# Positions loaded in two halves and loads reordered in the prologue of a Hyena filter with a maxout FFN

## The chip, the cores and the metric

The kernel runs on one core of one Trainium2 chip. The metric is the device time of one execution in microseconds (us), lower being better. All arrays are float32.

## The reference

The program is a Hyena long convolution followed by a feed-forward layer with three maxout branches. B = 4, S = 12544, D = 128, filter order 64, hidden width 768.

```python
h_filt = (np.maximum(pos_emb @ w1, 0.0) @ w2) * np.exp(-0.01 * pos)[:, None]
u = x * v
y = irfft(rfft(u, 2 * S) * rfft(h_filt, 2 * S), 2 * S)[:, :S]       # along the sequence
x = (x * y).reshape(B * S, D)
h = np.maximum(np.maximum(x @ moe_w1, x @ moe_w2), x @ moe_w3)
out = h @ moe_w_out
```

`pos_emb` is 12544 x 64. The decay, `exp(-0.01 pos)`, is zero in float32 from position 82 x 128 on, so only the first NH = 82 blocks of 128 positions (two halves of HH = 41 blocks) enter the filter.

## The kernel before

The program is written out by hand: the order of the calls in the source is the order of the instructions on each engine, and a tile's reader waits for its writer. Its stages are:

- a **prologue**, which makes the filter's hidden layer: relu of positions times w1, times the decay;
- 16 **quads** that transform four hidden channels each, then 32 quads that transform the units of batch 0, with the raw double-precision FFN weights turned into float32 on VectorE beside them;
- the filter's spectrum, stored to DRAM, and batch 0's convolution;
- a main loop of the FFN over tiles of batch 0, 1 and 2, with the convolution of the next batch in between, and a last stage for batch 3.

The change lies in the prologue. What happens there, with lines of the kernel before:

- **Positions.** `pos` (in the memory of `specH`) has 128 partitions: 64 filter inputs for the first 41 blocks and, below them, the same 64 for the other 41. Eight loads (L290 to L295), in pieces of 10 or 11 whole blocks, alternate between SP's and ACT's queues. Each partition's piece is one run of 5 KB or more.
- **Small constants on POOL's queue** (L282 to L289): the decay `win`, `eye`, the reversal `back`, and w1 twice (`w1_sb`).
- **Warm-up** (`warm_up`, L299): TensorE multiplies zeros, 22 rounds and later 3 more. One round is two matmuls, which the trace records as four.
- **The window** (`window_back`, L305): TensorE transposes `win` by `eye`; ACT copies it to `winT` in four pieces; TensorE multiplies by `back`, which reverses and splits it into even and odd positions; ACT copies the result to `winr`.
- **The relu groups** (loop at L903): `mlp_in(i)` (L321) is 32 matmuls into one of two PSUM tiles `pm`, for 16 of the 128 positions of every block, beginning with the highest. Groups 0 to 3 take positions 127 to 64, groups 4 to 7 take 63 to 0. `mlp_out(i)` (L333) is two VectorE instructions per group, relu times `winr`, and frees that `pm` for group i + 2. One relu-group matmul gives two records in the trace, so a group is 64 records.
- **Units.** `u_load` (L349) brings 4 channel rows of x and v (two loads of 196 KB in runs of 392 B) on SP's queue, `u_mul` (L359) multiplies them on VectorE, and `turn2` (L877) transposes two units on TensorE (`pst`), with one ACT copy (`uT`). Units 0 and 1 are turned behind group 7.
- **Raw FFN weights.** `load_raw` (L198) fills one of two buffers `raw` with half a weight matrix; `convert` (L211) is a list of 12 VectorE instructions, dealt out by `some` (L863) between the quads. The first two halves are loaded by SP, the others by POOL.
- **Order on SP's queue before:** four position loads; the first raw half (four loads); units 0 and 1; the second raw half; units 2 to 5. Later unit loads wait for buffers of units that have been turned. ACT's queue carries four position loads and, after the window, `f1h`, `w2` twice and `f1q`, which the quads need.

Of the kernel before, what the change touches and what calls it, by code (L numbers as in the profile page):

```python
# [10 lines left out]
FP32 = mybir.dt.float32  # L11
# [5 lines left out]
P = 128  # L17
# [10 lines left out]
HH = NH // 2  # L28
# [63 lines left out]
def kernel(  # L92
# [15 lines left out]
    nc = tc.nc  # L108
    NG, _, _, B, NB = x.shape
    FO, S = posT.shape  # L110
# [18 lines left out]
    f1_d = nc.inline_tensor(f1_t, name="f1_const").ap()  # L129
    f1h_d = nc.inline_tensor(f1h_t, name="f1h_const").ap()  # L130
# [12 lines left out]
    f1q = const.tile([NB, 2, 2 * N1], FP32, name="f1q")  # L143
# [8 lines left out]
    def halves_mm(out, lhsT, rhs, start, stop):  # L152


        for h in range(2):
            nc.tensor.matmul(out[64 * h:64 * h + 64], lhsT[:, 64 * h:64 * h + 64], rhs,  # L156
                             start=start, stop=stop, skip_group_check=True)
# [37 lines left out]
    def scratch(name, bufs):  # L195
        return sml.tile([P, 2 * HF], I32, tag=name, name=name, bufs=bufs)[:]

    def load_raw(i, h, eng):  # L198
        r = scratch("raw", 2)
        if i < 3:  # L200
            src = (moe_w1, moe_w2, moe_w3)[i].bitcast(I32).rearrange("(g c) f -> c g f", c=GC)
            for c in range(GC):
                eng.dma_start(r[c * NG:(c + 1) * NG],
                                  src[c][:, h * 2 * HF:(h + 1) * 2 * HF])
        else:
            src = moe_w_out.bitcast(I32).rearrange("(c p) d -> p c d", p=P)
            eng.dma_start(r.rearrange("p (c d) -> p c d", c=NF // 2),
                              src[:, h * NF // 2:(h + 1) * NF // 2, :])
        return r
# [47 lines left out]
    sml = fin.enter_context(tc.tile_pool(name="sml", bufs=1))  # L257
    mps = ExitStack()
    fps = mps.enter_context(tc.tile_pool(name="fps0", bufs=2, space=PSUM))
# [2 lines left out]

    specH = pin.tile([P, N1, 2, FO], FP32, name="specH")
    pos = specH[:].rearrange("p k r f -> p (k r f)")[:, 0:HH * P]
    posv = pos.rearrange("f (n p) -> f p n", p=P)
    hs = spec[0:64 + HH].rearrange("p k r d -> p (k r d)")[:, 0:FO * P].rearrange(
        "n (f r t) -> n f r t", r=2, t=64)
    w1_sb = sml.tile([P, FO], FP32, name="w1_sb")
    w2_in = sml.tile([P, D], FP32, name="w2_in")
    w2x = pin.tile([P, D], FP32, name="w2x")  # L270
    win = sml.tile([64 + HH, P], FP32, name="win")
    winT = sml.tile([P, 2, 64 + HH], FP32, name="winT")
    winr = sml.tile([64 + HH, 2, 64], FP32, name="winr")
    back = sml.tile([P, 2, 64], FP32, name="back")
    f1h = sml.tile([64 + HH, 2, 2 * N1], FP32, name="f1h")
    warm = sml.tile([P, 256], FP32, name="warm")
# [9 lines left out]
    nc.gpsimd.dma_start(eye[:], eye_d)  # L286
    nc.gpsimd.dma_start(back[:].rearrange("p r t -> p (r t)"), back_d)
    for h in range(2):
        nc.gpsimd.dma_start(w1_sb[64 * h:64 * h + 64], w1[:, :])  # L289
    cuts = (0, 11, 21, 31, HH)  # L290
    for j, (lo_, hi_) in enumerate(zip(cuts, cuts[1:])):
        for h in range(2):
            (nc.scalar if (h + j) % 2 else nc.sync).dma_start(
                pos[64 * h:64 * h + 64, lo_ * P:hi_ * P],
                posT[:, (h * HH + lo_) * P:(h * HH + hi_) * P])  # L295
    for r in range(2):
        nc.scalar.copy(winT[:, r, 0:64], warm[:, 0:64])

    def warm_up(n):  # L299

        ps = fps.tile([P, 1024], FP32, tag="cv", name="pw")
        for _ in range(n):
            halves_mm(ps[:, 0:256], warm[:, 0:P], warm[:], True, True)

    def window_back():  # L305
        pw = fps.tile([P, 1024], FP32, tag="cv", name="pw")
        nc.tensor.transpose(pw[:, 0:64 + HH], win[:], eye[0:64 + HH, 0:64 + HH])
        for r in range(2):
            for h in range(2):
                c = 64 * (h ^ r)  # L310
                nc.scalar.copy(winT[:, r, c:c + HH], pw[:, 64 * h:64 * h + HH])
        for r in range(2):
            nc.tensor.matmul(pw[0:64 + HH, 512 + 64 * r:576 + 64 * r], winT[:, r], back[:, r],
                             start=(r == 0), stop=True, skip_group_check=True)
        nc.scalar.copy(winr[:].rearrange("n r t -> n (r t)"), pw[0:64 + HH, 512:512 + P])

    def w2_order():
        nc.scalar.copy(w2x[:].rearrange("f (c g) -> f c g", c=GC),
                       w2_in[:].rearrange("f (g c) -> f c g", c=GC))

    def mlp_in(i):  # L321

        ps = pms[i % 2]
        for q in range(8):
            for r in range(2):
                for h in range(2):
                    c = 64 * (h ^ r)
                    nc.tensor.matmul(  # L328
                        ps[c:c + HH, 512 * r + q * FO:512 * r + (q + 1) * FO],
                        posv[64 * h:64 * h + 64, P - 1 - 2 * (8 * i + q) - r, :],  # L330
                        w1_sb[64 * h:64 * h + 64], start=(q == 0), stop=True,
                        skip_group_check=True)
    def mlp_out(i):  # L333
        v = pms[i % 2][0:64 + HH].rearrange("n (r t f) -> n r f t", r=2, t=8)
        for r in range(2):
            nc.vector.scalar_tensor_tensor(
                out=hs[:, :, r, 8 * i:8 * i + 8], in0=v[:, r], scalar=0.0,
                in1=winr[:, r, None, 8 * i:8 * i + 8].to_broadcast([64 + HH, FO, 8]),
                op0=ALU.max, op1=ALU.mult)
# [4 lines left out]
    def pools(b, u):  # L344
        if b == 0:
            return inp0 if u % 2 else inp
        return inp if u < EARLY or u % 4 < 3 else inq

    def u_load(b, u):  # L349
        c, g0 = divmod(u, NG // 4)  # L350
        ts = []
        for src in (xr, vr):
            t = pools(b, u).tile([P, 4, NB], FP32, tag=f"u{len(ts)}", name="ut")
            nc.sync.dma_start(
                t[:], src[4 * g0:4 * g0 + 4, :, c, b, :].rearrange("g p n -> p g n"))
            ts.append(t)
        us[u] = ts

    def u_mul(u):  # L359
        a, v = us[u]  # L360
        nc.vector.tensor_tensor(out=a[:], in0=a[:], in1=v[:], op=ALU.mult)  # L361

    def turn(u, ps):
        a, _ = us.pop(u)
        for i in range(4):
            nc.tensor.transpose(ps[0:NB, i * P:(i + 1) * P], a[:, i, :], eye[:])  # L366
# [369 lines left out]
    def up(i, f, tag="hid", bufs=3):  # L736
        rhs = gs[i][:].rearrange("d p n -> d (p n)")
        h = (hidp if tag == "hid" else lp).tile([P, N], FP32, tag=tag, name="hid", bufs=bufs)
        pa = next(hbanks)
        halves_mm(pa[:, 0:N], w_sb[1][:, f * P:(f + 1) * P], rhs, True, True)  # L740
        nc.scalar.activation(h[:], pa[:, 0:N], Relu)  # L741
        pb = next(hbanks)
        halves_mm(pb[:, 0:N], w_sb[2][:, f * P:(f + 1) * P], rhs, True, True)
        nc.vector.tensor_tensor(out=h[:], in0=h[:], in1=pb[:, 0:N], op=ALU.max)  # L744
        return h
# [114 lines left out]
    jobs = [(i, h) for i in range(4) for h in range(2)]  # L860
    raws, todo = [], []
# [15 lines left out]
    def turn2(u):  # L877

        t = utp.tile([NB, 8, 2, 64], FP32, tag="uT", name="uT")
        ps = fps.tile([P, 1024], FP32, tag="cv", name="pst")  # L880
        for v in range(2):
            turn(u + v, ps[:, 512 * v:512 * v + 512])
        nc.scalar.copy(t[:], ps[0:NB, :].rearrange("n (s t r) -> n s r t", s=8, r=2))
        uts[u] = t
# [2 lines left out]
        ps = fps.tile([P, 1024], FP32, tag="cv", name="ps1")  # L887
        first_halves(ps, lhs, table, dst, nc.scalar.copy)

    warm_up(22)  # L890
    window_back()
    warm_up(3)
    nc.scalar.dma_start(f1h[:], f1h_d)
    nc.scalar.dma_start(w2_in[0:FO], w2[:, :])
    nc.scalar.dma_start(w2_in[FO:P], w2[:, :])
    nc.scalar.dma_start(f1q[:], f1_d)
    raws.append(load_raw(*jobs[0], nc.sync))
    u_load(0, 0)
    u_load(0, 1)
    raws.append(load_raw(*jobs[1], nc.sync))  # L900
    for u in range(2, 6):
        u_load(0, u)
    for i in range(9):  # L903
        if i < 8:
            mlp_in(i)
        if i:
            mlp_out(i - 1)
        if i in (4, 5):
            u_mul(i - 4)
        if i == 7:  # L910
            turn2(0)
    w2_order()
    mps.close()
    fps = fin.enter_context(tc.tile_pool(name="fps", bufs=4, space=PSUM))
    for f in range(0, FO, 4):
        quad([hs[:, f + i] for i in range(4)], (f1h[:, 0], f1h[:, 1]), specH[:, :, :, f:f + 4])
        u, k = divmod(f // 4, 4)
# [11 lines left out]
    for u in range(0, NU, 2):  # L929
        t = uts.pop(u)  # L930
# [201 lines left out]
    for n, (b, i) in enumerate(tiles[:LAST]):  # L1132
# [10 lines left out]
        for f in range(NF):  # L1143
# [9 lines left out]
            h = up((b, i), f)  # L1153
# [40 lines left out]
    for i in range(0, NT, 2):  # L1194
        h = {}
        X, Y = banks if i % 4 == 0 else banks[::-1]
        for j, (name, f) in enumerate(ORDER):
            n = int(name[1]) - 1
# [64 lines left out]
```

## Time and profile before

| what | value |
|---|---|
| time, median of 3 runs | 2282.13 us (2281.03 to 2283.14) |
| the profiled execution's own time | 2286.24 us |
| its span, first to last instruction | 2284.5 us |
| busy: PE, DVE, ACT, POOL | 99%, 68%, 51%, 38% of the span |
| relu groups on TensorE | start 16.12 us, end 35.47 us |
| first quad on TensorE | starts 37.58 us |
| DMA in the first 30 us | 140 to 243 GB/s in steps of 5 us |

PE is TensorE's matmul side, PEld its weight loads, DVE VectorE, ACT ScalarE, POOL GpSimd, SP the engine that issues most transfers. SPq, ACTq and POOLq are the DMA issues on these engines. Times in the trace count from the first instruction of the span. The chain of waits follows the execution back from its last instruction; the step "issue" in it is time in which an engine waited for nothing that the profile shows. DMA share is the mean busy share of the 16 DMA engines, and can pass 1 where packets overlap.

### The profile page before, as it was taken

What the parts mean: (1) busy time and instruction counts of PE and PEld (TensorE: products, weight loads), DVE (VectorE), ACT (ScalarE), POOL (GpSimd) and SP (SyncE); (2) the same over time, 40 slices, a digit from 0 to 9 for tenths busy, and PEclk for the clock granted to TensorE, in tenths of its full rate; (3) what the DMA queues carried; (4) which work ended last, traced back from release to release, by engine and by line L of the source; (5) the groups of instructions that cost most, each with busy time, mean ns of one, the idle gap of its engine ahead of it and who ended that gap; (6) DMA issues with size and microseconds to landing.
All of it is one profiled execution on the core that took longest, in us unless ns stands there. A gap on an engine that the chain in (4) does not pass through costs nothing.

```text
span 2284.5 us, 68468 instructions
## 1 busy us (share of the span) xinstructions
PE 2256.9 (99%) x27855; PEld 1377.3 (60%) x27855; DVE 1561.3 (68%) x2854; ACT 1174.9 (51%) x2125; POOL 878.6 (38%) x1087
## 2 busy tenths in 40 slices
PE   8999999999999999999999999999999999999998
PEld 7989866655555556655555556655555556666665
DVE  5579867668787757657878756767878854544443
ACT  2688844456666534456666534456666622222222
POOL 2045434323333333423333334423333326666666
PEclk9999999999999999999999999999999999999999
DMA  8778989799999689879999889779999732222221
GB/s 182 188 220 278 303 178 182 141 217 245 238 220 245 181 171 174 164 186 250 238 234 239 206 162 186 160 174 254 234 241 238 199 86 56 56 68 64 62 56 22
DMA packets 473269, 411.03 MB, mean 180 GB/s; under 512 B 327865, under 2 KB 374426, under 8 KB 472954
## 3 DMA queue, kind: packets, MB, share of 16 engines
q1 hardware_dynamic: 445954, 329.48, 63.9%
q0 software_dynamic: 26288, 75.47, 11.0%
q8 instruction: 219, 3.59, 0.7%
q10 hardware_dynamic: 712, 1.70, 0.3%
q14 instruction: 96, 0.79, 0.1%
HBM read 262.84 MB, written 84.67 MB: 152 GB/s over the span
## 4 chain that ended last, share of the span: by engine, by line
PE 96%; DMA 1%; DVE 1%; issue 1%; ACT 0%; POOL 0%; SPq 0%; POOLq 0%; DVEq 0%; ACTq 0%
PE hps L156 44%; PE ops L156 19%; PE ops L804 6%; PE cps L413 5%; PE cps L156 4%; PE ps L156 3%; PE cps L474 3%; PE ps L165 3%; PE cps L484 3%; PE sps L1010 2%; PE gps L992 2%; PE last L156 1%; PE pst L366 1%; PE pm L328 1%; DMA back<-back_const 0%
## 5 line engine op out<-in xcount | busy, mean ns | idle before, releaser
L156 PE MATMUL hps<-gt,w_sb 128*64 128x392 f32 x6144 | 1150.7, 494 | 0.7 <-DVE gt L731 0.7
L741 ACT ACTIVATE hid<-hps 128x392 f32<-128x392 f32 x768 | 383.8, 500 | 703.3 <-PE hps L156 686.8
L156 PEld LDWEIGHTS hps<-gt,w_sb 128*64 128x64 f32 x6144 | 430.7, 137 | 422.0 <-issue 385.8
L744 DVE TENSOR_TENSOR hid<-hid,hps 128x392 f32<-128x392 f32 x768 | 428.3, 558 | 334.0 <-PE hps L156 325.6
L156 PE MATMUL ops<-hid,wo_sb 128*64 128x392 f32 x2304 | 480.0, 492 | 0.0
L526 POOL TENSOR_TENSOR cb<-cb,xs 128x512 f32<-128x512 f32 x135 | 174.1, 1290 | 462.6 <-DVE xs L523 345.8
L156 PEld LDWEIGHTS ops<-hid,wo_sb 128*64 128x64 f32 x2304 | 171.8, 137 | 207.4 <-issue 199.4
L426 DVE TENSOR_TENSOR spec<-cps,high 128x360 f32<-128x360 f32 x188 | 140.9, 790 | 127.2 <-ACT high L422 127.2
L499 DVE TENSOR_TENSOR cb<-cps,eo 128x512 f32<-128x512 f32 (+1 forms) x288 | 175.3, 650 | 74.0 <-ACT eo L496 74.0
L759 POOL DMA_DIRECT2D out_dram<-ot x96 | 75.4, 785 | 343.9 <-ACT ot L757 296.5
L514 ACT ACTIVATE xs<-cb 32x512 f32<-32x512 f32 x270 | 169.5, 628 | 20.5 <-DVE cb L499 11.5
L515 ACT COPY xs<-cb 32x512 f32<-32x512 f32 x270 | 166.3, 616 | 3.2
L422 ACT COPY high<-cps 128x360 f32<-128x360 f32 x94 | 75.0, 798 | 179.7 <-PE cps L413 145.9
L413 PEld LDWEIGHTS cps<-f1q,uT 98*64 98x64 f32 x3008 | 131.2, 138 | 29.3 <-issue 23.7
L530 DVE TENSOR_TENSOR xs<-cb 128x256 f32<-128x256 f32 x270 | 140.9, 567 | 9.2 <-POOL cb L526 9.0
L413 PE MATMUL cps<-f1q,uT 98*64 98x90 f32 x3008 | 135.5, 242 | 1.9 <-DVE uT L397 1.5
L382 POOL COPY planes<-ut 128x784 uint16<-128x784 uint16 x90 | 76.3, 848 | 155.0 <-DVE ut L361 141.3
L507 POOL DMA_DIRECT2D zd<-cb x135 | 92.8, 687 | 64.5 <-DVE cb L499 56.9
L156 PEld LDWEIGHTS cps<-f4p,even 90*64 90x64 f32 x1552 | 89.5, 138 | 35.0 <-issue 32.6
L828 POOL DMA_DIRECT2D out_dram<-o x128 | 77.7, 612 | 49.6 <-DVE o L821 47.9
L156 PE MATMUL cps<-f4p,zt 90*64 90x49 f32 x1552 | 96.3, 222 | 0.1
L156 PE MATMUL cps<-f4p,even 90*64 90x49 f32 x1552 | 95.0, 220 | 0.0
(143 smaller groups left out, 3149.4 us busy)
## 6 DMA issues: line engine op xcount, KB each, us to landing
ht<-hd SPq DMA_DIRECT2D x264, 256.0 KB, 6.7
wt<-wq_const SPq DMA_DIRECT2D x144, 256.0 KB, 6.2
zd<-cb POOLq DMA_DIRECT2D x135, 256.0 KB, 6.0
zt<-zd SPq DMA_DIRECT2D x384, 90.0 KB, 2.9
sq<-spec SPq DMA_DIRECT2D x264, 128.0 KB, 6.9
ut<-in_xr_dram SPq DMA_DIRECT2D x128, 196.0 KB, 4.1
ut<-in_vr_dram SPq DMA_DIRECT2D x128, 196.0 KB, 4.3
xT<-in_x_dram SPq DMA_DIRECT2D x256, 98.0 KB, 3.3
```

Source lines behind the costliest of these rows:

```text
L156: nc.tensor.matmul(out[64 * h:64 * h + 64], lhsT[:, 64 * h:64 * h + 64], rhs, start=start, stop=stop, skip_group_check=True)
L413: nc.tensor.matmul(ps[64 * c:64 * c + 64, 256 * i + h * N1:256 * i + (h + 1) * N1], t[:, 2 * ((at + i) % 8) + h].rearrange("n r t -> n (r ...
L426: nc.vector.tensor_tensor(out=spec[:, :, a, at:at + n], in0=v[:, 1], in1=high, op=op)
L499: nc.vector.tensor_tensor(out=cb[:, a, lo:hi], in0=ps[:, lo:hi], in1=eo[:, lo:hi], op=op)
L507: nc.gpsimd.dma_start(zd[b][2 * z:2 * z + 2].rearrange("k c t a f -> (k c t) a f"), zss.pop(z))
L514: nc.scalar.mul(xs[at:at + 32], xt[at + 32:at + 64], -1.0)
L515: nc.scalar.copy(xs[at + 32:at + 64], xt[at:at + 32])
L526: nc.gpsimd.tensor_tensor(out=xts[g], in0=xts[g], in1=xs[:], op=ALU.add)
L530: nc.vector.tensor_tensor(out=ab[:, q], in0=y[:, 0], in1=y[:, 1], op=(ALU.subtract, ALU.add)[q])
L741: nc.scalar.activation(h[:], pa[:, 0:N], Relu)
L744: nc.vector.tensor_tensor(out=h[:], in0=h[:], in1=pb[:, 0:N], op=ALU.max)
L804: nc.tensor.matmul(ps[64 * c:64 * c + 64, 0:H2], w, rhs[:, H2 * c:H2 * c + H2], start=start, stop=True, skip_group_check=True)
```

## The change

- The position loads are cut otherwise: first positions 64 to 127 of every block, then 0 to 63, each in four loads (blocks 0 to 20 and 21 to 40 of both halves). A contiguous run in them is 64 positions, 256 B.
- w1 is loaded ahead of the positions, one copy on SP's and one on ACT's queue, instead of on POOL's.
- The warm-up is 16 rounds in one piece.
- `window_back` is split: `window_turn` (transpose and the copies to `winT`) stands behind group 0 on TensorE, the rest behind group 1. The loads of `f1h`, `w2` and `f1q` follow it on ACT's queue.
- `winr` is gone; the window is copied twice, into the two `raw` buffers. Groups 0 to 4 read the first, groups 5 to 7 the second. So the first raw half can be loaded only behind the relu of group 4, the second behind that of group 7.
- SP's queue: positions; units 0 and 1; behind the relu of group 4 the first raw half and units 2 to 5; behind the last relu the second raw half.

```diff
--- before.py
+++ after.py
@@ -262,6 +262,7 @@
 
     specH = pin.tile([P, N1, 2, FO], FP32, name="specH")
     pos = specH[:].rearrange("p k r f -> p (k r f)")[:, 0:HH * P]
+    posn = pos.rearrange("f (n p) -> f n p", p=P)
     posv = pos.rearrange("f (n p) -> f p n", p=P)
     hs = spec[0:64 + HH].rearrange("p k r d -> p (k r d)")[:, 0:FO * P].rearrange(
         "n (f r t) -> n f r t", r=2, t=64)
@@ -270,7 +271,8 @@
     w2x = pin.tile([P, D], FP32, name="w2x")
     win = sml.tile([64 + HH, P], FP32, name="win")
     winT = sml.tile([P, 2, 64 + HH], FP32, name="winT")
-    winr = sml.tile([64 + HH, 2, 64], FP32, name="winr")
+    winrs = [scratch("raw", 2).bitcast(FP32)[0:64 + HH, 0:P].rearrange(
+        "n (r t) -> n r t", r=2) for _ in range(2)]
     back = sml.tile([P, 2, 64], FP32, name="back")
     f1h = sml.tile([64 + HH, 2, 2 * N1], FP32, name="f1h")
     warm = sml.tile([P, 256], FP32, name="warm")
@@ -286,13 +288,14 @@
     nc.gpsimd.dma_start(eye[:], eye_d)
     nc.gpsimd.dma_start(back[:].rearrange("p r t -> p (r t)"), back_d)
     for h in range(2):
-        nc.gpsimd.dma_start(w1_sb[64 * h:64 * h + 64], w1[:, :])
-    cuts = (0, 11, 21, 31, HH)
-    for j, (lo_, hi_) in enumerate(zip(cuts, cuts[1:])):
-        for h in range(2):
-            (nc.scalar if (h + j) % 2 else nc.sync).dma_start(
-                pos[64 * h:64 * h + 64, lo_ * P:hi_ * P],
-                posT[:, (h * HH + lo_) * P:(h * HH + hi_) * P])
+        (nc.scalar if h else nc.sync).dma_start(w1_sb[64 * h:64 * h + 64], w1[:, :])
+    for p0 in (64, 0):
+        for j, (lo_, hi_) in enumerate(((0, 21), (21, HH))):
+            for h in range(2):
+                (nc.scalar if (h + j) % 2 else nc.sync).dma_start(
+                    posn[64 * h:64 * h + 64, lo_:hi_, p0:p0 + 64],
+                    posT[:, (h * HH + lo_) * P:(h * HH + hi_) * P].rearrange(
+                        "f (n p) -> f n p", p=P)[:, :, p0:p0 + 64])
     for r in range(2):
         nc.scalar.copy(winT[:, r, 0:64], warm[:, 0:64])
 
@@ -302,17 +305,21 @@
         for _ in range(n):
             halves_mm(ps[:, 0:256], warm[:, 0:P], warm[:], True, True)
 
-    def window_back():
-        pw = fps.tile([P, 1024], FP32, tag="cv", name="pw")
+    pw = fps.tile([P, 1024], FP32, tag="cv", name="pw")
+
+    def window_turn():
         nc.tensor.transpose(pw[:, 0:64 + HH], win[:], eye[0:64 + HH, 0:64 + HH])
         for r in range(2):
             for h in range(2):
                 c = 64 * (h ^ r)
                 nc.scalar.copy(winT[:, r, c:c + HH], pw[:, 64 * h:64 * h + HH])
+
+    def window_back():
         for r in range(2):
             nc.tensor.matmul(pw[0:64 + HH, 512 + 64 * r:576 + 64 * r], winT[:, r], back[:, r],
                              start=(r == 0), stop=True, skip_group_check=True)
-        nc.scalar.copy(winr[:].rearrange("n r t -> n (r t)"), pw[0:64 + HH, 512:512 + P])
+        for winr in winrs:
+            nc.scalar.copy(winr.rearrange("n r t -> n (r t)"), pw[0:64 + HH, 512:512 + P])
 
     def w2_order():
         nc.scalar.copy(w2x[:].rearrange("f (c g) -> f c g", c=GC),
@@ -332,6 +339,7 @@
                         skip_group_check=True)
     def mlp_out(i):
         v = pms[i % 2][0:64 + HH].rearrange("n (r t f) -> n r f t", r=2, t=8)
+        winr = winrs[i > 4]
         for r in range(2):
             nc.vector.scalar_tensor_tensor(
                 out=hs[:, :, r, 8 * i:8 * i + 8], in0=v[:, r], scalar=0.0,
@@ -887,28 +895,31 @@
         ps = fps.tile([P, 1024], FP32, tag="cv", name="ps1")
         first_halves(ps, lhs, table, dst, nc.scalar.copy)
 
-    warm_up(22)
-    window_back()
-    warm_up(3)
-    nc.scalar.dma_start(f1h[:], f1h_d)
-    nc.scalar.dma_start(w2_in[0:FO], w2[:, :])
-    nc.scalar.dma_start(w2_in[FO:P], w2[:, :])
-    nc.scalar.dma_start(f1q[:], f1_d)
-    raws.append(load_raw(*jobs[0], nc.sync))
-    u_load(0, 0)
-    u_load(0, 1)
-    raws.append(load_raw(*jobs[1], nc.sync))
-    for u in range(2, 6):
+    warm_up(16)
+    for u in range(2):
         u_load(0, u)
     for i in range(9):
         if i < 8:
             mlp_in(i)
+        if i == 0:
+            window_turn()
+        if i == 1:
+            window_back()
+            nc.scalar.dma_start(f1h[:], f1h_d)
+            nc.scalar.dma_start(w2_in[0:FO], w2[:, :])
+            nc.scalar.dma_start(w2_in[FO:P], w2[:, :])
+            nc.scalar.dma_start(f1q[:], f1_d)
         if i:
             mlp_out(i - 1)
         if i in (4, 5):
             u_mul(i - 4)
+        if i == 5:
+            raws.append(load_raw(*jobs[0], nc.sync))
+            for u in range(2, 6):
+                u_load(0, u)
         if i == 7:
             turn2(0)
+    raws.append(load_raw(*jobs[1], nc.sync))
     w2_order()
     mps.close()
     fps = fin.enter_context(tc.tile_pool(name="fps", bufs=4, space=PSUM))
```

## The prediction

> **What bounds the kernel now.** First the page: its chain of waits gives TensorE 96% of the span, so time is lost or won where TensorE stands still. The change touches only the prologue, so next the same chain in order of time, cut to the first 120 us (start, length, engine, tile, line, count):
>
> ```profile
> 14.75 1.45 PE pw L156 x12
> 16.19 2.90 PE pm L328 x98
> 19.09 1.86 issue
> 20.95 3.73 PE pm L328 x120
> 24.68 1.65 issue
> 26.33 3.45 PE pm L328 x119
> 29.78 1.65 issue
> 31.43 4.04 PE pm L328 x119
> 35.47 1.02 PE pst L366 x8
> 36.49 0.02 issue
> 36.51 1.02 ACT uT L883
> 37.53 0.04 issue
> 37.58 8.90 PE ps L165 x224
> ```
>
> The eight relu groups (pm, 512 matmul records, 64 a group) begin at 16.19 and end at 35.47. Three gaps of 1.65 to 1.86 us, 5.16 us together, stand in them with no releaser. After 37.58 the chain is TensorE without a gap up to 116.56, but for one of 1.50 us at 57.63. What ends the gaps shows in the DMA view of half a microsecond inside the second one's approach, 23.5 to 24.0 us, and of 32.5 to 33.0 us:
>
> ```profile
> q1 hardware_dynamic: 211, 0.08, 121.6%
> q8 instruction: 1, 0.02, 16.2%
> ...
> q8 instruction: 1, 0.02, 12.0%
> ```
>
> Queue q8 brings TensorE's program. Its packets start at 18.3, 23.5, 29.0 and 32.5 us; TensorE resumes 2.4 to 2.8 us after each of the first three, and exactly 128 matmul records (the timeline's x128) run between two gaps. From a resumption to the next block's packet it is 2.6 us while loads fill the engines, but 1.1 us at 32.5, when nothing else moves. So a block takes 5.1 to 5.4 us under load and about 1.1 + 2.3 = 3.4 us without, against 3.5 to 3.7 us that its 128 records last. The windows show the two states (PE, PEld, DVE, ACT, POOL busy, clock, DMA share, GB/s):
>
> ```profile
> 26.00:28.00 2.00, 1.67 (x75) 1.67 (x76) 1.05 (x2) 0.00 (x0) 0.00 (x0) 1.00 1.00 234
> ...
> 32.00:34.00 2.00, 2.00 (x85) 2.00 (x81) 1.49 (x3) 0.00 (x0) 0.00 (x0) 0.50 0.03 8
> ```
>
> The start at 16.19 has its own cause: warm-up, window and loads end together. Landing times: position loads up to 13.2 us after issue, w1 11.3 us after 3.94 and 4.5 us (15.2 to 15.9), eye at about 12.8, back at about 14.1.
>
> [...] Here the unit loads, in runs of 392 B, moved 1230 packets and 234 GB/s in the window above, while the positions' 4.5 KB packets moved 215 GB/s from 6 to 10 us[...] 256 B runs alone are not seen in the trace. [...]
>
> **The change part by part.**
>
> *Positions by halves.* The same 2.69 MB now goes in 8 loads of 256 B runs, 10,496 packets; the first four groups need the first 5,248. Price from below: 256/392 of the 26.5 ns that a 392 B packet cost (3,620 packets in 24 to 30 us on 16 engines), 17.3 ns; from above that 26.5 ns itself. I take 20 ns: 6.6 us a half. From the first movement at 2.2 us, with 0.8 us for POOL's constants between and 1 us to land, the first half is there at 10.4 (8.9 to 12.5), the second at 17 (15 to 21.4).
>
> *w1 ahead.* Two loads of 16 KB leave POOL's queue and go first on SP and ACT, landing near 3 us instead of 15.9. The position loads behind each move by one issue, about 0.6 us, already in the 2.2.
>
> *Warm-up cut* from 25 rounds to 16: 36 records gone. It ends near 8.7 (12 records ran up to 4 us, then 11 per us), ahead of the positions, so nothing is gained or lost on the path.
>
> *Window turned between groups.* Its transpose stands behind group 0, so it can't hold that back; but TensorE runs in order, and a late eye now holds group 1. Eye at 12.8 and back at 14.1 as before; both may come 1 to 2 us earlier[...]. ACT gets one more copy of the window, 0.27 us, before the constants f1h, w2 and f1q; those are needed only at the first quad, 16 us later, so it is hidden.
>
> *Raw weights and units 2 to 5 later.* SP's order becomes: positions, 4 loads of units 0 and 1, then (behind the relu of group 4) 4 raw loads and 8 unit loads, then (behind the last relu) 4 raw loads. DMA falls silent from about 22 us until that release; two instruction blocks can use it. All else on SP queues behind the two raw waits; the next unit loads were released only by the turn of unit 0 anyway.
>
> *Walking it.* A group is 64 x 27.3 ns = 1.75 us (3.45 us per 128); its relu is 1.29 us and must free pm two groups later. Group 0 10.4 to 12.15; eye 12.8, transpose to 13.1; group 1 to 14.85; back to 15.4; window copy, 15.8; relu 0 to 17.1. Group 2 from 17.15. Counting records from the start, the first block boundary fell near record 91 and the block after it ended at record 219, the first gap; with the shorter warm-up 91 is 27 records into group 0 (11.2 us) and 219 is 22 into group 2 (17.75). The first fetch took 6.6 us (14.3 to 20.95), so 17.8: no stall. Group 2 ends 18.95, group 3 20.7. Group 4 stops after 22 records, at 21.3, until 17.8 + 5.4 = 23.2, a stall of 1.9, and ends 24.35; group 5 26.1. The next fetch, half in quiet, comes at 26.6 to 28.6 against 26.7; I take 0.5 us of stall. Group 6 28.4, group 7 30.15, turn of units 0 and 1 31.2, its copy 32.25. Before: 37.58. **Gain 5.3 us.**
>
> *Given back and given on top.* Raw and unit loads (2.3 MB, some 10 us at 230 GB/s) now run from 25.7 to about 37, beside the first quads, where DMA was at a third. A quad takes 1.24 us per 32 records, 4.96 us a block, against 5.1 to 5.4 for a loaded fetch: 0.3 us lost. DVE's conversion starts near 31 with its first raw tile landed at 29; the second lands near 37, about 1 us after DVE asks, which DVE absorbs, as turn 2 is the only thing TensorE wants of it there. Eye coming sooner: half of its 1 us, 0.5. From 46 us on the unit loads are released by TensorE's own progress and move with it. Sum: 5.3 - 0.3 + 0.5 = **5.5 us faster**. The profiled execution (span 2284.5, 2286.24 with what lies around) would become 2280.7; it stands 4.1 above the median of 2282.13, so I forecast 2276.6. A measurement tells some 0.2% of this kernel, 4.6 us, from no change.
>
> **The rivals.**
>
> *Fetch never stalls* in the relu groups (loads done by 20 us, eye early): another 1.9 + 0.5 us and 0.7 from eye, 8.5 us: 2273.6. For it speaks the fetch at 32.5; against, the second half and units 0 and 1 still fill the engines when the block for group 4 is asked for.
>
> *The loads only change places.* With 26.5 ns a packet the first half lands at 12.5 and the second at 21.4, units 0 and 1 at 25, so every fetch is a loaded one, and the deferred loads stretch fetches in the quads and delay DVE's raw tiles. Walked likewise, quads start near 35 with up to 1.5 us lost behind: 1 to 2.5 us faster, 2280.3. For it: DMA share is 0.96 to 1.28 from 2 to 30 us, and DVE later waits for units 12 times (11.8 us in all), with about 2 us in hand before TensorE's turns.
>
> *Short runs become the bound*, the slower side: group 4 waits for the second half. Behind it stand four groups, 7 us, and one fetch gap, 1.7, so the gain is gone when it lands at 26.8, and the loss passes 4.6 us at 31.4, that is at (31.4 - 4.0) x 16 / 10,496 = 42 ns a packet. For it: no such run is in the trace[...]. Against: it would be 1.6 times the 392 B packet for fewer bytes. Then about 2288.
>
> *The split does nothing*, because w1, eye and back, not positions, set 16.19: group 0 would start at 14 to 15; a gain of 1.5 to 3 us, inside no change.
>
> **How the numbers follow.** The walk, with its bounds, 0.48; no stall 0.12; loads change places or the split does little 0.30; short runs bound 0.10. The walk's own range is 3.5 to 7.5 us, with a fifth of it under 4.6. Faster by over 0.2%: 0.39 + 0.12 + a little of the third, 0.54. Within: 0.37. Slower: 0.09. Range: from 2273.2, past the no-stall case, to 2282.0, past the third case; the slow one is left out.
>
> **What would show it.** Right: pm starting at 10 to 11 us, the transpose near 12 to 13, one gap of about 2 us in group 4, the first quad near 32, a position load landing by 8 to 9 us after issue, DMA silent for some microseconds before 26. Wrong: pm starting after 13, or group 4 released by a position load; gaps of 1.7 us at every 128 records; a first gap among the quads, or DVE waiting for raw or units long enough that a turn waits for it; the first quad later than 34.

## The result, and the profile after

The change made the kernel slower, by 0.2%: 2286.68 us (median of 22 runs) against 2281.89 us for the kernel before (22 runs), a ratio of 1.0019 with a 95% interval of 1.0013 to 1.0025. Forecast were 2276.6 us and a range from 2273.2 to 2282.0.

The profiled execution of after took 2288.33 us, its span 2286.5. The chain of waits of after in order of time (start, length, what), with its first and its deciding stretch:

```profile
2.28 9.88 DMA specH<-in_pos_emb_dram
12.16 0.14 issue
12.30 1.71 PE pm L335 x54
...
18.10 0.90 PE pm L335 x24
19.00 3.09 issue
22.09 3.73 PE pm L335 x127
25.82 0.76 issue
26.58 6.33 PE pm L335 x212
...
35.02 8.90 PE ps L165 x224
...
51.33 8.47 DMA raw<-in_moe_w_dram
...
62.67 0.49 DVE ut L369
63.15 0.14 issue
63.29 1.95 PE pst L374 x8
65.23 4.34 PE ps L165 x64
69.58 1.01 PE pst L374 x8
70.58 2.63 PE ps L165 x64
```

Three things are to be seen. Group 0 starts at 12.30, earlier than before, and one long fetch gap (3.09 us) and a short one (0.76) stand where three stood. The first quad starts at 35.02: the prologue itself did become shorter. Then, at 51.33, the chain leaves TensorE for a raw-weight load, goes through VectorE's conversion to a product of a unit, and comes back to TensorE only at the turn of units 4 and 5 at 63.29. That turn takes 1.95 us and the two quads behind it 4.34, against 1.01 and 2.63 for the next ones.

The waits of TensorE in after, 34 to 70 us (who waited, for whom, us in total, times, longest):

```profile
PE pst L374 <- DVE ut L369: 4.3, 1, 4.3
```

In before no such wait is there, and VectorE hardly waits for raw halves in the same stretch (in after 10.5 us in two waits):

```profile
DVE ta L224 <- DMA raw<-in_moe_w_dram: 2.0, 1, 2.0
```

VectorE's timeline shows why (start, length, operation; in brackets the idle time ahead and what ended it):

```profile
46.57 0.36 DVE L224 TENSOR_SCALAR ta<-raw 128x384 int32<-128x384 int32 x1 [6.78 <-DMA raw<-in_moe_w_dram]
...
59.92 0.36 DVE L224 TENSOR_SCALAR ta<-raw 128x384 int32<-128x384 int32 x1 [3.70 <-DMA raw<-in_moe_w_dram]
...
62.31 0.35 DVE L235 TENSOR_SCALAR tb<-raw 128x384 int32<-128x384 int32 x1
62.58 0.56 DVE L369 TENSOR_TENSOR ut<-ut 128x392 f32<-128x392 f32 x1
```

VectorE stood 6.78 us for the second raw half, which SP had issued from 36.78 to 39.85 behind eight unit loads. The fourth half goes into the same buffer, so it can be loaded only when the second has been read, which was so at 49.3. POOL issued it at 49.86, right behind the landing of a unit's load at 49.82, which the profile names as the last of what it waited for. It ran beside the `wt` loads (filter matrices that are read at about 120 us), which SP issued from 48.19, and took 8.47 us. The product of unit 4 (L369) stands behind eight instructions of that half's conversion.

The windows of after (PE, PEld, DVE, ACT, POOL busy, clock, DMA share, GB/s) show the second price:

```profile
61.00:62.00 1.00, 0.00 (x0) 0.00 (x0) 0.93 (x3) 0.00 (x0) 0.00 (x0) 0.96 0.00 0
62.00:63.00 1.00, 0.00 (x0) 0.00 (x0) 0.96 (x4) 0.00 (x0) 0.04 (x1) 0.50 0.00 0
...
68.00:69.00 1.00, 1.00 (x20) 1.00 (x19) 1.00 (x4) 0.64 (x1) 0.00 (x0) 0.63 1.25 268
69.00:70.00 1.00, 1.00 (x21) 0.89 (x18) 0.97 (x4) 0.37 (x1) 0.00 (x0) 1.00 0.15 31
```

TensorE idles from 59.0; 2.9 us on, at 61.9, the granted clock falls to 0.50, and it stays there until 68.7, 5.4 us after work has come back. By the timeline the turn's eight matmuls then last 1.95 us and not 1.08, the pair of quads 4.41 and not 2.70: 2.6 us on top of the 4.3.

### The profile page after: what moved, and what is told of

Its sections match the earlier page's. It is cut to its first block, busy times and chain, and to the rows that moved or that the text cites. A ratio compares the mean times of both kernels' runs of the same rounds, so it can differ in the third digit from the quotient of the medians.

```text
span 2286.5 us, 68402 instructions
## 1 busy us (share of the span) xinstructions
PE 2255.6 (99%) x27819; PEld 1376.4 (60%) x27819; DVE 1560.5 (68%) x2854; ACT 1175.0 (51%) x2126; POOL 877.3 (38%) x1085
## 3 DMA queue, kind: packets, MB, share of 16 engines
q8 instruction: 219, 3.59, 0.7%
## 4 chain that ended last, share of the span: by engine, by line
PE 96%; DMA 1%; DVE 1%; issue 0%; ACT 0%; POOL 0%; SPq 0%; POOLq 0%; DVEq 0%; ACTq 0%
PE hps L156 44%; PE ops L156 19%; PE ops L812 6%; PE cps L421 5%; PE cps L156 4%; PE ps L156 4%; PE cps L482 3%; PE cps L492 3%; PE ps L165 2%; PE sps L1021 2%; PE gps L1003 2%; PE last L156 1%; PE pst L374 1%; PE pm L335 1%; DMA specH<-in_pos_emb_dram 0%
```

## The experiments

Each kernel ran beside runs of the kernel before on the same chip, and its ratio is to those. The profiles give two more marks: the first quad, and the first matmul of the filter's spectrum (gps), which is the end of the quads. Each row has one profile.

| kernel | median us | ratio (95%) | first quad | gps starts | quads last |
|---|---|---|---|---|---|
| before, first profile | 2281.89 | 1 | 37.58 | 117.4 | 79.8 |
| after | 2286.68 | 1.0019 (1.0013 to 1.0025) | 35.02 | 120.3 | 85.3 |
| e1, before again | 2282.84 | 0.9998 (0.9990 to 1.0006) | 36.52 | 115.7 | 79.2 |
| e2, second raw half first | 2283.16 | 1.0002 (0.9994 to 1.0010) | 34.46 | 117.5 | 83.0 |
| e3, loads as before | 2282.27 | 1.0003 (0.9994 to 1.0011) | 34.54 | 113.8 | 79.3 |
| e4, deferral alone | 2286.02 | 1.0015 (1.0009 to 1.0022) | 34.09 | 118.7 | 84.6 |
| e5, warm turn | 2285.82 | 1.0018 (1.0010 to 1.0025) | 35.00 | 118.3 | 83.3 |
| e6, whole positions | 2287.44 | 1.0018 (1.0012 to 1.0025) | 35.76 | 120.7 | 84.9 |
| e7, wt late | 2282.29 | 0.9998 (0.9990 to 1.0007) | 35.57 | 114.4 | 78.8 |
| e8, fewer conversions | 2282.22 | 0.9997 (0.9989 to 1.0006) | 35.00 | 114.5 | 79.5 |
| e9, e3 with both edits | 2281.27 | 0.9995 (0.9986 to 1.0003) | 35.32 | 113.3 | 78.0 |
| e10, before with both edits | 2281.30 | 0.9995 (0.9987 to 1.0003) | 36.27 | 114.3 | 78.0 |
| e12, after with both edits | 2281.31 | 0.9994 (0.9986 to 1.0002) | 35.13 | 113.2 | 78.1 |
| e13, e12 again | 2281.34 | 0.9994 (0.9986 to 1.0003) | 34.99 | 113.4 | 78.4 |

**e1.** No edit.

> The kernel before, unchanged, for a second profile: the first one was taken of an execution 4.1 us above its median. Both theories expect the times of before within 0.5 us. If the fetch gap of 1.50 us at 57.63 was particular to that execution, it is missing or shorter here; the relu gaps (5.16 us) should be within 1 us of what they were, and the first quad at 37 to 38 us.

The chain of waits of this second profile of before:

```profile
29.01 1.10 issue
30.11 3.46 PE pm L328 x115
33.56 0.27 issue
...
36.52 8.90 PE ps L165 x224
...
56.58 0.91 issue
57.48 3.94 PE ps L165 x95
```

Gaps in the relu groups were shorter (about 4.1 us in all) and the first quad came at 36.52, so 1.1 us of what the first profile offered for saving was particular to it (37 to 38 had been expected). The gap near 57 is there in both, 0.91 here.

**e4, the deferral alone, and e3, all but the deferral.** In e4 the kernel before gets only this (and the window copies in `raw`, as in the change):

```diff
-    raws.append(load_raw(*jobs[0], nc.sync))
     u_load(0, 0)
     u_load(0, 1)
-    raws.append(load_raw(*jobs[1], nc.sync))
-    for u in range(2, 6):
-        u_load(0, u)
...
+        if i == 5:
+            raws.append(load_raw(*jobs[0], nc.sync))
+            for u in range(2, 6):
+                u_load(0, u)
...
+    raws.append(load_raw(*jobs[1], nc.sync))
```

> The kernel before with the deferral alone: the window copied into the raw buffers, the first raw half and units 2 to 5 behind the relu of group 4, the second raw half behind the last; positions in whole blocks, w1, warm-up and window as before. Late-raw theory: the relu groups lose one or two of their three gaps (2 to 4 us sooner at the first quad, 34 to 35.5), then VectorE waits 5 to 8 us for the second raw half and TensorE stalls 3 to 5 us at the turn of units 4 and 5, with half clock behind; time 2284 to 2288. Rival, short runs cost the time: 2278 to 2280.

> The changed kernel with all raw and unit loads in the order of before on SP's queue, held by nothing (the window in its own tile); the positions by halves, w1 ahead and the turned window stay. Late-raw theory: no stall at the turn of units 4 and 5; every fetch in the relu groups is a loaded one, three gaps of 1.5 to 3 us, first quad at 36 to 38 us; time within 1.5 us of before (2281 to 2283). Rival, short runs cost the time: the first quad later than 38 and the time 2284 or more.

Waits in e4, 34 to 70 us:

```profile
DVE ta L224 <- DMA raw<-in_moe_w_dram: 9.1, 2, 6.3
...
PE pst L369 <- DVE ut L364: 2.7, 1, 2.7
```

The deferral alone does both things that the whole change does: the first quad comes sooner than in any other profile (34.09; one relu gap of 1.34 us is left and one of 0.23), and the quads last 84.6 us. It carries most of the loss, 1.0015. Without it, in e3, the loss is gone (1.0003) and the quads last 79.3. Short runs of positions do not cost the time.

One expectation for e3 failed: with the unit loads held by nothing, three gaps of 1.5 to 3 us and a first quad at 36 to 38 were expected, and the gaps were 1.39, 0.20 and 0.30 us, the first quad at 34.54. So the earlier first quad does not need the deferral. Either part of the change brings it alone (e3, e4), and the two together bring no more (35.02). Differences below 0.8 us tell nothing here: e9 has the prologue of e3 and its first quad is at 35.32.

**e2, the second raw half ahead of units 2 to 5.** The load moves by one line, and groups 5 to 7 read a window in a tile of its own, so that the buffer is free behind the relu of group 4.

```diff
         if i == 5:
             raws.append(load_raw(*jobs[0], nc.sync))
+            raws.append(load_raw(*jobs[1], nc.sync))
             for u in range(2, 6):
                 u_load(0, u)
...
-    raws.append(load_raw(*jobs[1], nc.sync))
```

> The changed kernel, with the second raw half released together with the first, behind the relu of group 4, and ahead of units 2 to 5 (the window of groups 5 to 7 in a tile of its own). Late-raw theory (second raw half lands 6.8 us after VectorE asks, conversions run late, the products of units 4 and 5 stand behind them, TensorE waits 4.3 us at their turn and then runs at half clock): no wait for raw over 2 us, no stall at that turn, the stage of quads ends 5 to 7 us sooner than after, time 2279 to 2281. Rival, that the short position runs and the fetches at the start cost the time: first quad still near 35, and the time within 1 us of after, near 2286.

The time is that of before, so when this load is let go and its place on SP's queue decide. But time (2279 to 2281) and profile were expected to be better than they are. VectorE's waits in e2, 34 to 70 us, and below them the chain of waits near 57:

```profile
DVE ut L370 <- DMA ut<-in_vr_dram: 7.1, 2, 6.6
DVE ta L224 <- DMA raw<-in_moe_w_dram: 1.9, 2, 1.4
```

```profile
56.46 2.61 issue
59.07 4.12 PE ps L165 x59
```

The wait has passed from raw tiles to units, which now come last, and the fetch gap near 57 has grown to 2.61 us, with half clock behind it (0.50; 59 records in 4.12 us, where in e1 at 1.00 63 took 2.70). The quads last 83.0 us, only 2.3 less than in after.

**e6, positions in whole blocks, the rest as changed.**

```diff
-    for p0 in (64, 0):
-        for j, (lo_, hi_) in enumerate(((0, 21), (21, HH))):
...
+    cuts = (0, 11, 21, 31, HH)
+    for j, (lo_, hi_) in enumerate(zip(cuts, cuts[1:])):
```

> The changed kernel with the positions loaded in whole blocks as before (runs of 5 KB), all else as changed. Late-raw theory: group 0 starts at 14 to 15.5 us, later than the 12.3 of after, but the fetches are shorter; first quad at 34 to 36, as after within 1.5 us; the stall at the turn of units 4 and 5 stays (3 to 5 us), time 2285 to 2288. Rival, short runs cost the time: 2280 to 2283.

Group 0 started at 16.61, later than expected, 4.3 us behind after, yet the first quad came only 0.7 us behind, because the groups then ran without the long gap. TensorE's timeline in e6:

```profile
16.61 2.23 PE L334 MATMUL pm<-w_sb,specH 64*41 64x64 f32 x64 [5.67 <-DMA specH<-in_pos_emb_dram]
...
23.12 7.48 PE L334 MATMUL pm<-w_sb,specH 64*41 64x64 f32 x279 [1.68 <-DVE spec L343]
```

The loss stayed whole (1.0018). Halving the positions gives little and costs nothing that can be measured.

**e8, fewer conversions ahead of the products, and e7, the wt loads later.** No load of raw or units moves in e8; e7 moves only loads that are read at about 120 us.

```diff
 e8
-        some(2 if u < 2 and k < 2 else 3)
+        some(2)
 e7
-    wf = {g: load_dir(g, 0) for g in range(3)}
-    wi = {g: load_dir(g, 1) for g in range(3)}
     for u in range(0, NU, 2):
...
+        if u == 20:
+            wf = {g: load_dir(g, 0) for g in range(3)}
+            wi = {g: load_dir(g, 1) for g in range(3)}
```

> The changed kernel with two conversion instructions behind each of the 16 filter quads in place of two or three, 32 and not 44; the 12 go behind the later quads. Every load stays where the change has it, so raw tiles land as late. Theory that what turns a late raw tile into lost time is VectorE's order, with the products of units 4 and 5 behind conversions: these products come before the late tile is asked for, the stall at the turn goes, time 2279.5 to 2282.5. Rival, that DMA is full and units themselves are late: the stall at that turn or the next stays over 2 us, time 2285 or more.

> The changed kernel with the six loads of wt (256 KB each), issued by SP near 48 us and first read at 119 us, put behind the last unit loads (near 103 us). Theory that the third POOL raw half lands late (8.5 us) because it runs beside them: that landing falls to 4 to 6 us, the stall at the turn falls from 4.3 to under 2 us, a fetch stall near 57 goes; time 2282 to 2284. Rival, that only the second raw half behind eight unit loads matters: VectorE's wait at 46.5 and the turn's stall stay over 3 us; time within 1 us of after.

(The half that the text of e7 calls POOL's third is the fourth of all, POOL's second.) VectorE's timeline in e8, and TensorE's:

```profile
46.19 0.36 DVE L224 TENSOR_SCALAR ta<-raw 128x384 int32<-128x384 int32 x1 [6.52 <-DMA raw<-in_moe_w_dram]
53.71 0.56 DVE L369 TENSOR_TENSOR ut<-ut 128x392 f32<-128x392 f32 x1
```

```profile
57.68 2.54 PE L165 MATMUL ps<-f1q,uT 98*64 98x90 f32 x59 [0.86 <-issue]
60.15 1.08 PE L374 MATMUL pst<-eye,ut 128*98 128x128 f32 x8
```

The second raw half is as late as in after (6.52 us of waiting), but the product of unit 4 is done at 54 and the turn at 60.15 waits for nothing. The loss is gone, 0.9997. In e7 VectorE still waits 6.0 us for the second half, but not for the fourth; the turn waits 0.34 and 0.24 us, and the loss is gone too, 0.9998. So the late tile, its collision with wt and VectorE's order all have to come together; taking away any one is enough for the time, though in e2 a part of the loss comes back in the profile as a late unit and a longer fetch gap.

**e5, TensorE kept busy through the stall.**

```diff
+        if u == 0:
+            ps = fps.tile([P, 1024], FP32, tag="cv", name="pw")
+            for _ in range(11):
+                halves_mm(ps[:, 0:256], warm[:, 0:P], warm[:], True, True)
         if u + 4 < NU:
             turn2(u + 4)
```

> The changed kernel with 11 rounds of zero matmuls (some 4 us at full clock) on TensorE just ahead of the turn of units 4 and 5, where it stood idle for 4.3 us. It leaves the wait and its cause in place. Theory that the stall is paid twice, as idle time and as half clock behind it: granted clock stays 1.0 through the turn and the two quads behind it, which take 2.7 us a pair and not 4.4, so the stage of quads ends about 2.5 us sooner than after relative to the turn; time 2283.5 to 2285. Rival, that only the wait counts: no gain, 2286 to 2288 (the added matmuls may even delay the turn).

TensorE's timeline in e5:

```profile
59.00 4.91 PE L156 MATMUL pw<-warm 128*64 128x256 f32 x43
63.84 1.11 PE L374 MATMUL pst<-eye,ut 128*98 128x128 f32 x8
64.89 2.70 PE L165 MATMUL ps<-f1q,uT 98*64 98x90 f32 x64
```

With no idle time the clock stays at 1.00 from 58 to 68 us, turn and quads take 1.11 and 2.70 us, and gps starts 2.0 us sooner than in after, though the turn itself came 0.6 later. That the slow quads are the clock's is shown. The median, 2285.82, lies above the 2283.5 to 2285 expected and does not tell it from after. A likely reason, not shown, is that 4.9 us of zero matmuls delay the turn in executions where the wait is shorter.

**e9, e10, e12, e13: both edits together.** e7's and e8's edits on e3, on before, and on after (twice).

> The changed kernel with the loads in the order of before (as in e3), two conversions behind each filter quad (as in e8) and the wt loads behind the last unit loads (as in e7). With the late raw tile, VectorE's order and the wt loads out of the way, what is left of the change is the earlier first quad. If that reaches the end: 2278 to 2280.5. If it is lost in the fetches under load, as e3's median suggests: 2281.5 to 2283.

> The kernel before with the same two edits behind the prologue (two conversions behind each filter quad, wt loads behind the last unit loads), nothing of the change. They take away the fetch stall near 57 us (0.9 to 1.5 us): 2280.5 to 2282.5. It is what e12 is to be compared with: if the change's prologue gives something, e12 is 1 to 3 us faster than this one; if not, the two are equal within 1 us.

> The changed kernel with both edits behind the prologue (e7 and e8 together). No stall at the turn of units 4 and 5, no fetch stall over 1 us near 57. First quad at 35, as after; stage of quads done at 111.5 to 113.5. If the earlier first quad reaches the end: 2279 to 2281, and faster than e10 by 1 to 2.5 us; if the deferred loads cost it elsewhere: 2281.5 to 2283.

> The same kernel as e12 a second time, since its interval, 0.9986 to 1.0002, does not tell it from before. If it gains what its profile shows (the main stage starts at 302.4 us, against 304.6 in the second profile of before), some 2 us: 2280 to 2281.5 and a ratio of 0.9990 to 0.9995. If that was chance: 0.9998 or more.

The four medians agree within 0.07 us. In e12 the first quad is 1.1 us ahead of e10's, and gps as well; the medians do not show even that, and the gain of 1 to 2.5 us over e10 that was held possible did not come. The 13 runs of each spread over 3.4 us (e10) and 2.6 us (e12), so a gain of 1 us is not excluded either. With what it did to VectorE taken away, the change is worth about 1 us in the profile and nothing that the times can tell. The kernels with both edits have the lowest medians, 0.7 to 1.9 us below the runs of before beside them. That is not the change's doing, for e10 has nothing of it; and each interval still holds 1, that of e13 too, though its median lies where a gain was expected.

## Why the prediction was wrong

*The step that failed* is the one that gave the late loads nothing: "the second lands near 37, about 1 us after DVE asks, which DVE absorbs, as turn 2 is the only thing TensorE wants of it there". It landed at 46.5, 6.8 us after VectorE asked (39.8). The relu of group 4 released the loads at 29.4 and not 25.7, and from there to the landing it took 17.1 us and not 11.3. The eight unit loads ahead of the half were in the forecast. What was not is that SP was issuing until 39.85, and that the third half (POOL, from 37.48) and the next unit loads (SP, from 39.95) moved beside it: 3.58 MB from 29.4 to 46.57, where 2.3 were counted, with 278, 249 and 222 GB/s in the windows from 34 to 46 us. Nor did the `wt` loads from 48.19 on, which held up the fourth half, stand in any term. And "the only thing TensorE wants of it there" left out what comes later: the turn of units 4 and 5 waits on VectorE too. In before its product was ready some 8 us ahead of the turn:

```profile
54.58 0.56 DVE L361 TENSOR_TENSOR ut<-ut 128x392 f32<-128x392 f32 x1
62.99 1.08 PE L366 MATMUL pst<-eye,ut 128*98 128x128 f32 x8
```

In after it ran at 62.58, and TensorE had been ready at 59.0. The right question of a late tile is not what reads it, but what stands behind its reader on the same engine, for as long as the lag lasts; e8, which changes only that, takes the loss away.

*The second price*, half clock behind a stall, was in no term. It adds 2.6 us to the 4.3, and e5 shows that it is the clock's.

*The gain* was right in kind (though, as e3 and e4 show, its parts do not add up) and too large: 5.3 us at the first quad were forecast against the first profile, where 2.6 came, and 1.5 against the second. Three terms: a packet of 256 B took 25 ns (5,074 on SP's and ACT's queues from 10 to 18 us, 16 engines), near the upper bound and not the 20 taken, so group 0 began at 12.30 and not 10.4. The first fetch was asked for at some 13.0 us, if the prediction's count of records holds (27 into group 0), and was over at 22.09: an estimated 9 us and not 6.6, and a gap of 3.09 where none was forecast. That a block is asked for where TensorE enters the one before it is the author's estimate, here and in the prediction; the profile shows when a block's packet moves, not when it was asked for. The second gap was 0.76 and not 1.9. That the boundaries fell at record 24 of group 2 and 127 on bears out the count by blocks of 128 (22 was forecast). One sum was off by itself: 2.2, 0.8, 6.6 and 1 us make 10.6 and not 10.4 for the first half, and its bounds 9.7 and 12.7; nothing hangs on it. Eye landed at about 10.7 and back at 12.3, some 2 us sooner than in before (12.8 and 14.1), so the 1 to 2 us forecast were right; what brought them was not shown.

*The rivals.* "Short runs become the bound" named the right sign and the wrong cause: group 4 never waited for positions, and e6 keeps the loss without short runs. "The loads only change places" named DVE's raw tiles, with 1.5 us at most.

*The sum after the fact*, after against e1: first quad -1.5; quads +6.1, which are 4.3 of idle time, 2.6 of half clock and a fetch gap of 0.9 that is gone; then 0.8 up to the main stage, whose first matmul (hps) starts at 310.0 against 304.6: +5.4. Behind that mark the two take 1976.5 and 1976.4 us. The spans of the two differ by 5.5, so the sum closes for these two executions; the medians differ by 4.8. Not settled is how often the stall is shorter: after's 22 runs spread over 8 us (2282.66 to 2290.59), and only one of them has a profile, at 2288.33, 1.65 above the median.

## What to carry to other kernels

Before a load is put behind something, list the in-order engine that reads it and everything queued behind that reader until its lag is made up; the cost comes where another engine wants one of those (here 4.3 us of TensorE at the turn of units 4 and 5). Three stalls of 2.71 to 5.26 us on TensorE were paid a second time here, with 1.5 to 3.3 us at half clock (e4, after, e6), so price a stall with the slow work behind it. Where DMA is near full, as here from 34 to 58 us (222 to 310 GB/s in the windows of after), deferring loads can move the collision rather than remove it (in e2 from raw tiles to units, 7.1 us of waits), and the loads to move are those with slack to spare (here wt, read 70 us later; e7, 0.9998).

## What the runs showed of the hardware

Loads in runs of 256 B moved 161 to 168 GB/s from 10 to 16 us, against 215 for the same data in 4.5 KB packets (before, 6 to 10 us).

Behind a gap of 2.61 us (e2) TensorE's clock stood at 0.50, while behind 1.50 us in before and 0.91 in e1, near the same place, it stood at 1.00; but in the relu groups of before 0.50 stands from 21.6 to 25.0 us, behind a gap of 1.86, and from 31.8 to 35.2, behind one of 1.65, and behind the other gap of 1.65, from 26.33 on, 1.00. So in these runs length alone does not tell. Nor does it set the price, as the profiles with a stall at the turn of units 4 and 5 show (what turn and pair took above 1.08 and 2.70 us, and in e4 0.1 of the next turn):

| run | stall, us | clock at 0.50 | dearer by, us |
|---|---|---|---|
| e4 | 2.71 | 61.3 to 68.1 | 3.3 |
| after | 4.30 | 61.9 to 68.7 | 2.6 |
| e6 | 5.26 | 64.6 to 68.0 | 1.5 |

Where the windows give both ends of a stretch at 0.50 among the relu groups and the quads, it lasted 3.4 us (the two of before, e2 from 59.8 to 63.2, e6), 6.8 (after and e4 in the quads) or 13.7 (after, 17.5 to 31.2), whatever the gap. The relu groups hardly feel them: 128 of their records took 3.73 us in before from 20.95, most of it at 0.50, and 3.45 from 26.33 at 1.00.

The page of before counts 219 packets of queue q8 ("instruction"), 3.59 MB, beside 55,710 records of matmuls and weight loads, some 254 a packet; in after it is 219 beside 55,638. In after q8's packets start at 18.95 and 24.05 us, and TensorE resumes 3.1 and 2.5 us later (22.09 and 26.58); at the gap of 1.50 us in before it is 2.6 (56.5 and 59.12). For the gaps near 57 in e1 and e2 this is not shown.

By the count of records, and with the estimate of when it is asked for, a block of TensorE's program took some 9 us to arrive in after (13.0 to 22.09), beside loads in runs of 256 B, against the 5.1 to 5.4 estimated beside the unit loads of before.
